# Windowed attention and a highway layer on one core: the t bias in four pieces beside the shifted value matmuls, merged exponentials, masks and copies from block 7 on, and a new order table

## The chip, the core and the metric

The kernel runs on 1 core of a Trainium2 chip. The metric is the device time of one execution in microseconds. Engines named below: PE (TensorE matmul), DVE (VectorE), ACT (ScalarE), POOL (GpSimd) and SP (SyncE). Before the change, 13 runs had a median of 120.59 us, from 119.31 to 123.08.

## What is computed

Attention over a sliding window with four sink positions, for 4 batches, 8 heads, 768 positions and 64 columns a head; its output, as 3072 tokens of 512 columns, goes through one highway layer.

```python
scores = scale * np.matmul(q, k.transpose(0, 1, 3, 2))
is_sink = pos[None, :] < n_sink                       # n_sink = 4
rel = pos[:, None] - pos[None, :]
in_window = (rel >= 0) & (rel < window)               # window = 128
scores = np.where(is_sink | in_window, scores, -1e9)
a = softmax(scores);  x = np.matmul(a, v)             # x as [3072, 512]
H = np.maximum(x @ w_h, 0.0)
T = 1.0 / (1.0 + np.exp(-(x @ w_t + b_t)))
out = T * H + (1.0 - T) * x
```

## The kernel before

The tokens are cut into 24 blocks of 128, six to a batch. The keys of block n are held in a chunk that is shifted by 64 positions, so that a block needs its own chunk in full and a half of the chunk on either side. Every block n goes through the same steps, each named by a letter in the order table and defined in the table STEP (L652):

- Loads: q, k and v of a block come through POOL's queue (L112, L119, L126), 128 KB each. The first ones stand in a fixed list (L210 to L238), the two weight matrices wh_sb and wt_sb (512 KB each, L191) among them. The later ones are issued inside the step A: A:n issues v of n+4, q and k of n+6 (L636).
- Tq, Tk: PE transposes of q or k into a PSUM tile (L323); tq, tk (ACT) or tqV, tkV (DVE) copy them out (L328). From block 3 on, the transposes are made inside S of an earlier block and stand in unused columns of that block's score tile ("hosted", L607). In and after block 9 one ACT copy, tt (L335), takes out both.
- S: the scores, the block's own chunk (L376) and the two half chunks (L389), into two PSUM tiles of two banks, each holding half of the heads. From block M0 = 9 on they are one tile of four banks with a single buffer (L295).
- x0_, x1_: the exponential of each half (ACT, L398); from block 9 on one xx for both (L403). m0_, m1_ and mm multiply with the window's mask (DVE, L409).
- sk, es: scores of the sink positions and their exponential (PE L358, ACT L365).
- A: the value product into the PSUM tile av, of which there is one. First the shifted value matmuls (L434), 16 of 64x64 operands and 66 columns: they use only the two quarters of the PE array that connect the lower rows with the upper columns and the other way round. Then the block's own chunk (L453) and the sinks (L459).
- xh: reciprocal of the denominators and the normalized block (DVE, L467 and L472). X transposes it back into av (PE, L486); xT (ACT) or xTV (DVE) copies that out (L491), after which the next block's A may overwrite av.
- Mh and Mt: the products with w_h (L514) and w_t (L502), four matmuls of 512 columns, into one of two PSUM banks m0 and m1. Which bank the n-th user gets is written out in the string M_BANKS.
- u: the tanh of the t half (ACT, L507). d, U, e and o (DVE, L520, L526, L531, L536) combine the two; o also issues the store on SP. The last block is done in two halves (Ta, Ha, ..., pb).

The t bias b_t is added on PE: a product of a row of ones with the bias row opens the accumulation group of Mt. For blocks 0 to 7 it is one matmul over the full array just ahead of Mt (L499). From B0 = 9 on, the step A of block n begins with the bias of block n-1 (pe_bias, L440), two matmuls of 64x64 operands and 512 columns, in the two quarters that the shifted value matmuls leave free. ones_row holds the ones of the first kind, ones2 those of the second.

The whole order is written by hand, in one table ORDER (L676): every engine takes its instructions in the order of this table and waits only for what its operands need. A step that waits holds back everything behind it on its engine. wA are idle matmuls at the start, which keep PE active.

Of the kernel before, what the change touches and what calls it, by code (L numbers as in the profile page):

```python
# [8 lines left out]
FP16 = mybir.dt.float16  # L9
# [11 lines left out]
def kernel(  # L21
# [18 lines left out]
    nc = tc.nc  # L40
# [49 lines left out]
    B0 = 9  # L90
    M0 = 9
# [52 lines left out]
    ones2 = const.tile([P, P], FP16, tag="ones2")  # L144
# [48 lines left out]
    with tc.manual_schedule(engines={ENG.Pool, ENG.SP}):  # L193
# [16 lines left out]
        load_q(3)  # L210
        load_k(2)
        load_q(4)
        load_q(1)
        load_k(3)
        load_q(2)
        load_v(2)
        load_k(5)
# [6 lines left out]
        load_k(4)  # L224
        load_v(3)
        load_w(moe_w_h, wh_sb)
        load_q(5)
        load_k(6)
        load_w(moe_w_t, wt_sb)
        load_v(4)  # L230
        load_q(6)
        load_k(7)
# [29 lines left out]
    def bias_rows(_):  # L262
        nc.vector.memset(bt16, 0.0)
        nc.vector.memset(ones_row, 0.0)
        nc.vector.memset(ones_row[0:1, :], 1.0)
        nc.vector.tensor_copy(out=ones2, in_=ones_row)
        nc.vector.memset(ones2[HP:HP + 1, :], 1.0)
# [5 lines left out]
    def sink_ones(_):  # L273
# [6 lines left out]
        "010101010101010101010101010010100101001100101011010110101101"  # L280
# [146 lines left out]
    def pe_AB(n):  # L427
        av = av_tile(n)
        nxt = v_ring[vi(n + 1)]
        prv = v_ring[vi(n - 1 if n % NSC else n)]  # L430
        lo, hi = slice(0, HP), slice(HP, P)
        for j in range(H):
            for src, part, vt, h in ((lo, hi, nxt, j), (hi, lo, prv, (j + 4) % H)):
                nc.tensor.matmul(  # L434
                    av[part, h // 4, h % 4, 0:_AVN], lhsT=e_at(n, h)[src, P:EW],
                    rhs=vt[src, 65 * h:65 * h + _AVN], start=(h % 4 == 0), stop=False,
                    skip_group_check=True)

    def pe_bias(n):
        t_of[n] = m_tile()  # L440
        for rows in (slice(0, HP), slice(HP, P)):
            nc.tensor.matmul(t_of[n][rows, :], lhsT=ones2[rows, rows], rhs=bt16[rows, :],
                             start=True, stop=False, skip_group_check=True)

    def pe_A(n):
        if n >= B0:
            pe_bias(n - 1)
# [229 lines left out]
    mz0_:0 ma:0 na:0 Tq:0 na:1 Tk:0 tq:0 mz1_:0 tk:0 ma:1 wA:0 wA:0 Tk:1 mc:0 cv:0 tk:1 fa:0  # L677
    wA:0 wA:0 wA:0 S:0 cv:1 x0_:0 fb:0 x1_:0 wA:0 wA:0 wA:0 wA:0 Tq:3 m0_:0 fc:0 tq:3 wA:0 Tk:2
    tk:2 m1_:0 fd:0 wA:0 wA:0 wA:0 wA:0 Tq:1 A:0 tq:1 S:1 xh:0 sk:1 x0_:1 x1_:1 Tq:2 m0_:1 X:0
    sk:3 xTV:0 es:1 Tk:3 m1_:1 tq:2 tk:3 wA:1 A:1 es:3 S:2 xh:1 x0_:2 x1_:2 Tk:4 m0_:2 sk:2  # L680
    tkV:4 X:1 es:2 m1_:2 S:3 xT:1 A:2 x0_:3 Mh:1 x1_:3 xh:2 tq:4 d:1 X:2 tk:5 Mh:0 xTV:2 m0_:3
    Mh:2 d:0 m1_:3 S:4 d:2 Mt:0 x0_:4 x1_:4 m0_:4 A:3 u:0 m1_:4 Mt:1 tq:5 xh:3 tk:6 U:0 sk:4 u:1
    e:0 S:5 es:4 o:0 X:3 x0_:5 U:1 sk:5 xTV:3 e:1 A:4 x1_:5 m0_:5 o:1 tq:6 Mt:2 xh:4 tk:7 es:5
    u:2 m1_:5 X:4 S:6 xT:4 U:2 e:2 A:5 x0_:6 o:2 Mh:3 x1_:6 xh:5 tq:7 Mh:4 m0_:6 tk:8 m1_:6 X:5
    d:3 S:7 xT:5 d:4 A:6 x0_:7 Mh:5 xh:6 x1_:7 Mt:3 d:5 tq:8 tk:9 m0_:7 X:6 u:3 m1_:7 Mt:5 xT:6
    U:3 e:3 sk:7 o:3 u:5 Tq:9 es:7 U:5 Mt:4 tq:9 e:5 o:5 S:8 u:4 U:4 A:7 x0_:8 e:4 o:4 Mt:6
    x1_:8 xh:7 tq:10 Mh:6 m0_:8 tk:10 m1_:8 u:6 X:7 d:6 S:9 xT:7 U:6 A:8 e:6 xx:9 o:6 sk:9 xh:8
    Mh:7 es:9 tt:9 mm:9 Mt:7 d:7 X:8 u:7 S:10 xTV:8 U:7 A:9 e:7 xx:10 o:7 Mt:8 xh:9 tt:10 Mh:8
    mm:10 u:8 X:9 d:8 S:11 xT:9 U:8 A:10 e:8 xx:11 o:8 sk:11 xh:10 Mt:9 es:11 tt:11 mm:11 Mh:9
    u:9 X:10 d:9 S:12 xT:10 U:9 A:11 e:9 xx:12 o:9 Mt:10 xh:11 tt:12 Mh:10 mm:12 u:10 X:11 d:10  # L690
    S:13 xT:11 U:10 A:12 e:10 xx:13 o:10 sk:13 xh:12 Mt:11 es:13 tt:13 mm:13 Mh:11 u:11 X:12
    d:11 S:14 xT:12 U:11 A:13 e:11 xx:14 o:11 Mh:12 xh:13 tt:14 Mt:12 mm:14 X:13 d:12 u:12 S:15
    xT:13 U:12 e:12 xx:15 A:14 o:12 sk:15 xh:14 Mt:13 tt:15 mm:15 es:15 X:14 S:16 u:13 xTV:14
    U:13 A:15 xx:16 Mh:14 xh:15 tt:16 Mt:14 d:14 mm:16 Mh:13 u:14 U:14 sk:17 d:13 X:15 es:17
    S:17 xT:15 e:13 e:14 A:16 xx:17 o:13 o:14 Mt:15 xh:16 tt:17 Mh:15 mm:17 u:15 X:16 S:18 d:15
    xT:16 U:15 A:17 xx:18 e:15 o:15 Mh:16 xh:17 tt:18 Mt:16 mm:18 X:17 u:16 S:19 xTV:17 d:16
    A:18 xx:19 U:16 e:16 sk:19 xh:18 Mt:17 es:19 mm:19 tt:19 Mh:17 o:16 u:17 X:18 S:20 d:17
    xT:18 U:17 A:19 xx:20 e:17 o:17 Mh:18 xh:19 tt:20 Mt:18 mm:20 X:19 u:18 S:21 xTV:19 d:18
    A:20 xx:21 U:18 e:18 sk:21 o:18 Mt:19 es:21 xh:20 tt:21 Mh:19 mm:21 u:19 X:20 S:22 d:19
    xT:20 U:19 A:21 xx:22 e:19 o:19 Mh:20 xh:21 tk:24 Mt:20 mm:22 X:21 u:20 S:23 xTV:21 d:20  # L700
    A:22 xx:23 U:20 e:20 sk:23 xh:22 Mt:21 es:23 mm:23 X:22 u:21 Mh:21 xT:22 o:20 A:23 d:21 U:21
    Mt:22 xh:23 e:21 X:23 u:22 Mh:22 xTV:23 o:21 Ta:23 d:22 Ha:23 ua:23 U:22 e:22 Tb:23 da:23
    o:22 Hb:23 ub:23 db:23 ea:23 eb:23 pa:23 pb:23
# [43 lines left out]
```

## Time and profile before

| | us |
|---|---|
| median of 13 runs | 120.59 |
| the profiled execution | 120.56 |
| its span, first to last instruction | 118.5 |
| outside the span | 2.06 |
| first scores, S:1 | from 13.86 |
| S:5 | from 29.34 |
| S:9 | from 48.30 |
| last store's computation ends | 115.1 |

The PE clock was granted in full in all 40 slices but the last. The page's durations of PE instructions include the pipeline: a matmul of 512 columns is shown with 379 ns, but four in a row take 0.86 us. So two PE instructions that overlap in the list are the normal case, and start times say more than durations. DVE's and ACT's instructions overlap by about 0.08 and 0.10 us in the same way. "Idle before" in brackets is the time that an engine had nothing to do before an instruction, with what ended it. DMA queues carry 17.64 MB over the span; the mean time from issue to landing is 5.6 to 6.3 us for a tile of q, k or v.

### The profile page before, as it was taken

Reading aid. Unit: us, or ns where it says so; the run is one execution under the profiler, and the core shown is the slowest. Engines: PE = TensorE matmul, PEld = TensorE weight load, DVE = VectorE, ACT = ScalarE, POOL = GpSimd, SP = SyncE. Lnnn points to the kernel's source line nnn. Section 1 sums busy time; section 2 is a strip of 40 time slices with the busy share of each in tenths; the row PEclk is TensorE's granted clock in tenths of the full one; section 3 lists DMA queues with packets and bytes.
Section 4 is the critical chain, followed back from the end, with each engine's and each line's share of the span. In section 5 each row is a group of like instructions: output and inputs, shape, how many; then the busy total and the mean of one; then the engine's idle time right before and its main releaser. Section 6 shows DMA issues by size and latency. Waiting matters only on the chain.

```text
span 118.5 us, 4975 instructions
## 1 busy us (share of the span) xinstructions
PE 107.1 (90%) x2119; PEld 65.4 (55%) x2119; DVE 103.3 (87%) x254; ACT 87.4 (74%) x123; POOL 72.1 (61%) x97
## 2 busy tenths in 40 slices
PE   5998777999899999999999989999999999999920
PEld 1433555556655556755765556757656665565610
DVE  6889847588989897999999999879999999999990
ACT  2249397929978978979989969897888979783210
POOL 5999886859799129976959838887694320000000
PEclk9999999999999999999999999999999999999995
DMA  2999999999999969999999999999899995112132
GB/s 60 217 168 152 148 173 175 196 155 153 121 229 198 159 58 193 184 148 202 192 180 156 141 196 172 193 131 113 133 197 187 176 138 115 44 50 84 50 132 89
DMA packets 79848, 17.64 MB, mean 149 GB/s; under 512 B 75602, under 2 KB 76882, under 8 KB 79828
## 3 DMA queue, kind: packets, MB, share of 16 engines
q0 software_dynamic: 71888, 9.97, 134.6%
q1 hardware_dynamic: 6884, 7.12, 19.4%
q10 hardware_dynamic: 1056, 0.26, 1.4%
q8 instruction: 16, 0.26, 0.9%
q14 instruction: 4, 0.03, 0.1%
HBM read 21.01 MB, written 6.29 MB: 230 GB/s over the span
## 4 chain that ended last, share of the span: by engine, by line
PE 53%; DVE 23%; DMA 6%; ACT 6%; issue 5%; POOL 3%; DVEq 0%; ACTq 0%
PE m L514 11%; PE m L502 10%; DMA qsd<-in_q_dram 6%; PE av L453 6%; DVE xh L472 5%; PE av L434 5%; DVE otok L536 5%; DVE e L409 3%; PE sps L323 3%; PE av L486 3%; PE sps L389 3%; ACT e L398 3%; PE sps L376 3%; PE av L459 3%; DVE dd L520 3%
## 5 line engine op out<-in xcount | busy, mean ns | idle before, releaser
L126 POOL DMA_DIRECT2D v<-in_v_dram x26 | 22.0, 849 | 13.8 <-PE av L434 10.7
L403 ACT ACTIVATE e<-sps,ebias 128x1536 f16<-128x1536 f32 x15 | 23.1, 1541 | 3.8 <-PE sps L389 3.5
L409 DVE TENSOR_TENSOR e<-e,mask 128x768 f16<-128x768 f16 (+1 forms) x33 | 23.9, 732 | 2.2 <-ACT e L398 2.2
L112 POOL DMA_DIRECT2D qsd<-in_q_dram x23 | 20.8, 905 | 5.4 <-PE sps L323 5.4
L502 PE MATMUL m<-wt_sb,xT 128*128 128x512 f16 x92 | 23.6, 379 | 0.0
L514 PE MATMUL m<-wh_sb,xT 128*128 128x512 f16 x92 | 23.3, 379 | 0.0
L119 POOL DMA_DIRECT2D ksd<-in_k_dram x26 | 22.1, 853 | 1.0 <-DVE otok L536 0.6
L398 ACT ACTIVATE e<-sps,ebias 128x768 f16<-128x768 f32 x18 | 15.3, 898 | 5.1 <-PE sps L389 4.8
L507 ACT ACTIVATE u<-m 128x512 f16<-128x512 f32 x23 | 13.7, 596 | 6.7 <-PE m L502 6.5
L472 DVE TENSOR_TENSOR xh<-av,rec 128x512 f16<-128x512 f32 x24 | 16.6, 691 | 0.8
L536 DVE SCALAR_TENSOR_TENSOR otok<-xh,ee 128x512 f32<-128x512 f16 x23 | 15.8, 689 | 0.6
L520 DVE SCALAR_TENSOR_TENSOR dd<-m,xh 128x512 f16<-128x512 f32 x23 | 15.7, 685 | 0.0
L514 PEld LDWEIGHTS <-xT 128*128 128x128 f16 x92 | 8.7, 98 | 8.6 <-issue 0.4
L502 PEld LDWEIGHTS <-xT 128*128 128x128 f16 x92 | 8.7, 98 | 8.0
L335 ACT COPY tt<-sps 128x1024 f16<-128x1024 f16 x13 | 13.0, 997 | 0.0
L434 PE MATMUL av<-v,e 64*64 64x66 f16 x384 | 10.9, 193 | 0.9 <-DVE xT L491 0.3
L328 ACT COPY t<-sps 128x512 f16<-128x512 f16 x19 | 10.4, 590 | 1.6 <-PE sps L323 1.6
L434 PEld LDWEIGHTS <-e 64*64 64x64 f16 x384 | 9.8, 107 | 2.9 <-issue 2.0
L531 DVE TENSOR_TENSOR ee<-u,dd 128x512 f16<-128x512 f16 x23 | 10.0, 439 | 0.7
L453 PE MATMUL av<-v,e 128*128 128x66 f16 x192 | 10.4, 196 | 0.0
L486 PEld LDWEIGHTS <-xh 64*128 64x128 f16 x192 | 4.2, 95 | 9.5 <-DVE xh L472 6.8
L491 ACT COPY xT<-av 128x512 f16<-128x512 f16 x15 | 8.7, 581 | 1.0 <-PE av L486 0.7
(94 smaller groups left out, 171.5 us busy)
## 6 DMA issues: line engine op xcount, KB each, us to landing
out_dram<-otok SPq DMA_DIRECT2D x23, 256.0 KB, 3.6
qsd<-in_q_dram POOLq DMA_DIRECT2D x23, 128.0 KB, 5.6
ksd<-in_k_dram POOLq DMA_DIRECT2D x19, 128.0 KB, 6.3
v<-in_v_dram POOLq DMA_DIRECT2D x19, 128.0 KB, 5.8
wh_sb<-in_moe_w_h_dram POOLq DMA_DIRECT2D x1, 512.0 KB, 8.4
wt_sb<-in_moe_w_t_dram POOLq DMA_DIRECT2D x1, 512.0 KB, 9.0
ksd<-in_k_dram POOLq DMA_DIRECT2D x7, 64.0 KB, 5.7
v<-in_v_dram POOLq DMA_DIRECT2D x7, 64.0 KB, 5.9
```

The lines of the kernel that those rows point to most:

```text
L112: nc.gpsimd.dma_start(out=qsd, in_=q[b, :, c * P:(c + 1) * P, :].transpose([1, 0, 2]))
L119: nc.gpsimd.dma_start(out=ksd[rows], in_=k[b, :, s0:s0 + nr, :].transpose([1, 0, 2]))
L126: nc.gpsimd.dma_start(out=vt[rows, :, 0:D], in_=v[b, :, s0:s0 + nr, :].transpose([1, 0, 2]))
L398: nc.scalar.activation(out=e_tile(n)[:, g].rearrange("p a b c -> p a (b c)"), in_=s_tile(n, g)[:, :, 0:2 * EW], func=AF.Exp, bias=ebias, s ...
L403: nc.scalar.activation(out=e_tile(n).rearrange("p g a b c -> p (g a) (b c)"), in_=s_of[n][:, :, 0:2 * EW], func=AF.Exp, bias=ebias, scale= ...
L409: nc.vector.tensor_tensor(out=ev, in0=ev, in1=m.unsqueeze(1).to_broadcast([P, k, EW]), op=ALU.mult)
L434: nc.tensor.matmul(av[part, h // 4, h % 4, 0:_AVN], lhsT=e_at(n, h)[src, P:EW], rhs=vt[src, 65 * h:65 * h + _AVN], start=(h % 4 == 0), sto ...
L472: nc.vector.tensor_tensor(out=xh.rearrange("p (h d) -> p h d", d=D), in0=av_of.pop(n)[:, :, 0:D], in1=rec_of.pop(n).unsqueeze(2).to_broadc ...
L502: nc.tensor.matmul(t_of[n], lhsT=xT[:, kc, :], rhs=wt_sb[:, kc, :], start=False, stop=(kc == NOC - 1), skip_group_check=True)
L514: nc.tensor.matmul(hps, lhsT=xT[:, kc, :], rhs=wh_sb[:, kc, :], start=(kc == 0), stop=(kc == NOC - 1))
L520: nc.vector.scalar_tensor_tensor(out=dd, in0=h_of.pop(n), scalar=0.0, in1=xh_of[n], op0=ALU.max, op1=ALU.subtract)
L536: nc.vector.scalar_tensor_tensor(out=otok, in0=xh_of.pop(n), scalar=2.0, in1=ee_of.pop(n), op0=ALU.mult, op1=ALU.add)
```

## The change

- Bias: pe_bias and ones2 go. In the new table T_BESIDE block n of A names the block m whose bias is opened in it. The bias is cut in four pieces of 128 columns, each as two 64x64 matmuls, issued after the first, third, fifth and seventh pair of shifted value matmuls. It holds t of blocks 2 (in A:3), 0 (A:4), 4 (A:6), 6 (A:7), and n-1 for A:8 to A:23. Blocks 1, 3 and 5 keep the full-array matmul ahead of Mt. ones_row now holds the ones in row 0 for the first 64 columns and in row 64 for the others, which serves both kinds.
- M0 goes from 9 to 7: blocks 7 and 8 use the four-bank score tile, and so xx, tt and mm.
- The first loads on POOL stand in another order.
- ORDER is new, and with it the string M_BANKS.

```diff
-    B0 = 9
-    M0 = 9
+    T_BESIDE = {3: 2, 4: 0, 6: 4, 7: 6, 8: 7, 9: 8, 10: 9, 11: 10, 12: 11, 13: 12, 14: 13, 15: 14, 16: 15, 17: 16, 18: 17, 19: 18, 20: 19, 21: 20, 22: 21, 23: 22}
+    M0 = 7
...
-        load_q(3)
-        load_k(2)
-        load_q(4)
         load_q(1)
         load_k(3)
+        load_k(2)
+        load_k(6)
         load_q(2)
         load_v(2)
-        load_k(5)
+        load_q(3)
+        load_k(4)
+        load_v(3)
...
-        load_k(4)
-        load_v(3)
+        load_q(4)
+        load_k(5)
+        load_q(5)
+        load_v(4)
         load_w(moe_w_h, wh_sb)
-        load_q(5)
-        load_k(6)
         load_w(moe_w_t, wt_sb)
-        load_v(4)
+        load_k(7)
         load_q(6)
-        load_k(7)
         load_v(5)
...
         nc.vector.memset(ones_row, 0.0)
-        nc.vector.memset(ones_row[0:1, :], 1.0)
-        nc.vector.tensor_copy(out=ones2, in_=ones_row)
-        nc.vector.memset(ones2[HP:HP + 1, :], 1.0)
+        nc.vector.memset(ones_row[0:1, 0:HP], 1.0)
+        nc.vector.memset(ones_row[HP:HP + 1, HP:P], 1.0)
...
-        "010101010101010101010101010010100101001100101011010110101101"
+        "010101010100101101011010110101010110101100101011010110101101"
...
+        m = T_BESIDE.get(n)
+        if m is not None:
+            t_of[m] = m_tile()
         for j in range(H):
             for src, part, vt, h in ((lo, hi, nxt, j), (hi, lo, prv, (j + 4) % H)):
                 nc.tensor.matmul(
                     av[part, h // 4, h % 4, 0:_AVN], lhsT=e_at(n, h)[src, P:EW],
                     rhs=vt[src, 65 * h:65 * h + _AVN], start=(h % 4 == 0), stop=False,
                     skip_group_check=True)
-
-    def pe_bias(n):
-        t_of[n] = m_tile()
-        for rows in (slice(0, HP), slice(HP, P)):
-            nc.tensor.matmul(t_of[n][rows, :], lhsT=ones2[rows, rows], rhs=bt16[rows, :],
-                             start=True, stop=False, skip_group_check=True)
+            if m is not None and j % 2 == 0:
+                cols = slice(D * j, D * j + 2 * D)
+                for part in (lo, hi):
+                    nc.tensor.matmul(
+                        t_of[m][part, cols], lhsT=ones_row[part, part], rhs=bt16[part, cols],
+                        start=(j == 0), stop=False, skip_group_check=True)
 
     def pe_A(n):
-        if n >= B0:
-            pe_bias(n - 1)
         pe_AB(n)
```

The order tables are 461 and 456 steps long. Here are the stretches that the prediction speaks of: the start, up to S:5, and blocks 13 to 16.

```diff
-    mz0_:0 ma:0 na:0 Tq:0 na:1 Tk:0 tq:0 mz1_:0 tk:0 ma:1 wA:0 wA:0 Tk:1 mc:0 cv:0 tk:1 fa:0
-    wA:0 wA:0 wA:0 S:0 cv:1 x0_:0 fb:0 x1_:0 wA:0 wA:0 wA:0 wA:0 Tq:3 m0_:0 fc:0 tq:3 wA:0 Tk:2
-    tk:2 m1_:0 fd:0 wA:0 wA:0 wA:0 wA:0 Tq:1 A:0 tq:1 S:1 xh:0 sk:1 x0_:1 x1_:1 Tq:2 m0_:1 X:0
-    sk:3 xTV:0 es:1 Tk:3 m1_:1 tq:2 tk:3 wA:1 A:1 es:3 S:2 xh:1 x0_:2 x1_:2 Tk:4 m0_:2 sk:2
-    tkV:4 X:1 es:2 m1_:2 S:3 xT:1 A:2 x0_:3 Mh:1 x1_:3 xh:2 tq:4 d:1 X:2 tk:5 Mh:0 xTV:2 m0_:3
-    Mh:2 d:0 m1_:3 S:4 d:2 Mt:0 x0_:4 x1_:4 m0_:4 A:3 u:0 m1_:4 Mt:1 tq:5 xh:3 tk:6 U:0 sk:4 u:1
-    e:0 S:5 es:4 o:0 X:3 x0_:5 U:1 sk:5 xTV:3 e:1 A:4 x1_:5 m0_:5 o:1 tq:6 Mt:2 xh:4 tk:7 es:5
+    mz0_:0 ma:0 na:0 na:1 wA:0 wA:0 Tk:0 mz1_:0 Tq:0 tk:0 ma:1 tq:0 mc:0 Tk:1 cv:0 tk:1 fa:0
+    wA:0 wA:0 wA:0 S:0 fb:0 x0_:0 cv:1 x1_:0 wA:0 wA:0 wA:0 wA:0 Tq:1 m0_:0 tq:1 m1_:0 wA:0 wA:0
+    wA:0 Tk:2 Tk:3 tk:2 tkV:3 fc:0 wA:0 wA:0 S:1 A:0 x0_:1 fd:0 xh:0 x1_:1 Tq:2 sk:1 tq:2 m0_:1
+    es:1 m1_:1 Tq:3 X:0 tq:3 xTV:0 sk:3 S:2 es:3 sk:2 x0_:2 x1_:2 wA:1 wA:1 Tk:4 m0_:2 A:1 tkV:4
+    es:2 m1_:2 S:3 xh:1 x0_:3 X:1 xTV:1 x1_:3 m0_:3 A:2 tq:4 m1_:3 tk:5 xh:2 X:2 sk:4 xT:2 Mh:1
+    es:4 S:4 d:1 A:3 x0_:4 x1_:4 Mt:2 xh:3 tq:5 Mt:1 m0_:4 u:2 m1_:4 tk:6 U:2 Mh:0 u:1 U:1 X:3
+    d:0 S:5 xT:3 e:1 sk:5 x0_:5 o:1 A:4 es:5 m0_:5 x1_:5 Mh:2 xh:4 tq:6 Mt:0 m1_:5 tk:7 d:2 X:4
...
-    S:13 xT:11 U:10 A:12 e:10 xx:13 o:10 sk:13 xh:12 Mt:11 es:13 tt:13 mm:13 Mh:11 u:11 X:12
-    d:11 S:14 xT:12 U:11 A:13 e:11 xx:14 o:11 Mh:12 xh:13 tt:14 Mt:12 mm:14 X:13 d:12 u:12 S:15
-    xT:13 U:12 e:12 xx:15 A:14 o:12 sk:15 xh:14 Mt:13 tt:15 mm:15 es:15 X:14 S:16 u:13 xTV:14
-    U:13 A:15 xx:16 Mh:14 xh:15 tt:16 Mt:14 d:14 mm:16 Mh:13 u:14 U:14 sk:17 d:13 X:15 es:17
+    Mt:11 xh:12 tt:13 sk:13 mm:13 u:11 X:12 S:14 xT:12 U:11 es:13 xx:14 A:13 Mh:11 xh:13 tt:14
+    Mt:12 d:11 mm:14 sk:15 u:12 X:13 es:15 S:15 xTV:13 e:11 A:14 xx:15 U:12 o:11 Mt:13 xh:14
+    tt:15 Mh:12 mm:15 u:13 X:14 d:12 S:16 xT:14 e:12 A:15 xx:16 U:13 o:12 Mh:13 xh:15 tt:16
+    Mt:14 d:13 mm:16 X:15 u:14 Mh:14 xT:15 e:13 U:14 sk:17 d:14 S:17 es:17 o:13 A:16 xx:17 e:14
```

In the new table DVE has the copies tkV:3, tkV:4, tqV:9 and xTV of blocks 0, 1, 4, 6, 13, 17, 19, 21 and 23; before, tkV:4 and xTV of 0, 2, 3, 8, 14, 17, 19, 21 and 23.

## The prediction, made before the changed kernel ran

> **What bounds the kernel now.** I read the page from the top: the busy times, then the busy time by stretch, then the chain of waits, then the timeline of one engine at a time where these pointed.
>
> ```profile
> PE 107.1 (90%) x2119; PEld 65.4 (55%) x2119; DVE 103.3 (87%) x254; ACT 87.4 (74%) x123; POOL 72.1 (61%) x97
> ```
>
> No engine stands out, so a share of the span says little. The windows cut the run at DVE's first score mask (11.73 us), at 29.0 and at the reciprocals of blocks 9 and 23 (54.64, 108.99). Columns: stretch, length, busy us (instructions) of PE, weight loads, DVE, ACT, POOL, then PE clock, DMA, GB/s.
>
> ```profile
> 54.64:108.99 54.35, 53.56 (x1152) 33.79 (x1151) 51.85 (x101) 46.69 (x58) 28.71 (x37) 1.00 1.39 143
> 11.73:29.00 17.27, 15.01 (x324) 9.35 (x322) 12.12 (x27) 11.94 (x21) 13.60 (x17) 1.00 2.24 168
> 29.00:54.64 25.64, 24.76 (x530) 15.66 (x529) 23.39 (x51) 21.90 (x36) 19.50 (x25) 1.00 1.98 164
> ```
>
> DVE's idle time is 5.15 us in the start, 2.25 in the middle, 2.50 in the long regular part. PE records are pipelined, so PE's 0.8 us of idle in the last stretch is not all its slack. From 29 us on, the kernel is bound by PE and DVE together, and what can be won is idle time of both. DVE's timeline says where it lies (brackets: idle before, and who ended it).
>
> ```profile
> 22.02 0.21 DVE L467 RECIPROCAL rec<-av 128x8 f32<-128x8 f32 x1 [1.25 <-PE av L459]
> ...
> 45.37 0.29 DVE L526 TENSOR_SCALAR u<-u 128x512 f16<-128x512 f16 x1 [0.51 <-ACT u L507]
> ...
> 77.74 0.21 DVE L467 RECIPROCAL rec<-av 128x8 f32<-128x8 f32 x1 [0.93 <-PE av L459]
> ```
>
> **Part 1, the bias.** PE's timeline around block 9's shifted value matmuls (L434), and around block 19's:
>
> ```profile
> 53.33 0.38 PE L442 MATMUL m<-bt,ones 64*64 64x512 f16 x1
> 53.34 0.20 PE L434 MATMUL av<-v,e 64*64 64x66 f16 x2
> 53.34 0.38 PE L442 MATMUL m<-bt,ones 64*64 64x512 f16 x1
> 53.37 0.39 PE L434 MATMUL av<-v,e 64*64 64x66 f16 x14
> 53.70 0.43 PE L453 MATMUL av<-v,e 128*128 128x66 f16 x8
> ...
> 92.97 0.39 PE L442 MATMUL m<-bt,ones 64*64 64x512 f16 x2
> 93.12 0.45 PE L434 MATMUL av<-v,e 64*64 64x66 f16 x16
> ```
>
> At 53.33 the two bias halves and the value matmuls start within 0.01 us of each other and the full-array matmuls follow 0.37 later. So the four 64x64 quarters of the array already work at once. At 92.97 the bias runs while L434 waits for the copy of xT, which ACT's timeline has from 92.48 for 0.58 (to 93.06). For t of blocks 8 to 22, 15 pairs, the bias costs nothing today, and moving it gains nothing. What it costs as eight pieces of 128 columns: four 512-column matmuls take 0.86 in the chain, so 512 columns are 0.216 and a piece 0.054. Four on each quarter are 0.22, beside eight value matmuls per quarter that take 0.26 to issue: 0. If the two halves had to take turns, 8 x 0.054 = 0.43, that is 0.17 more a block. I take 0, by the row at 53.33.
>
> [...]
>
> Five full-array biases in front of Mt (L499, t of blocks 0, 2, 4, 6, 7) go: 5 x 0.216 = 1.08 us of PE, all before 52 us. The chain holds four L499 pieces (0.22, 0.22, 0.32, 0.38), so some of it counts; it is inside the walk below. A bias piece also waits for its m bank, and behind it in PE's queue stand the rest of that A step and the next product. I followed the bank string: the nearest readers are es:4 before A:3 and es:17 before A:16, each with a whole S step (0.7 us) between, against 0.35 for es. I take 0.
>
> **Part 2, merging blocks 7 and 8.** ACT: two half exponentials take 1.69 and two copies 1.07, merged 1.54 and 1.00, so 0.22 saved a block; ACT has slack, 0. DVE: two half masks occupy 0.93 until the next instruction, a merged one 0.87: 2 x 0.07 = 0.14 saved. Price: the first mask begins 0.64 later (after 1.54, not 0.90), and S:8 waits for tt:7, as the merged tile has one buffer. PE has two products queued between, so I take -0.14, with +0.6 as the other end.
>
> **Part 3, setup and copies on DVE.** The copy to ones2 and its memset go: 7.92 to 8.49, 0.57, less about 0.15 for the new one-row memset. DVE's early queue is full, so the first mask moves from 11.73 to 11.3. DVE takes 12 PSUM copies instead of 10: +2 x 0.34 = +0.67, one of them before 29 us.
>
> **Part 4, the start.** Chain: q1, fourth in POOL's queue, was issued at 5.54 and landed 7.31 later, at 12.85; PE sat idle for it. k2, second, was needed and there at 10.94. That is about 0.97 a place. Now q1 is first and k2 third (11.9). I walk the new order with the rows' durations, from 11.9: both k transposes and copies to 12.8; S:1 12.8 (was 13.86); its half exponentials end 15.1 (16.19); S:2 16.9 (17.82), ends of its exponentials 19.2 (20.19); S:3 19.5 (20.24), 22.1 (22.86). So the attention is about 0.9 us ahead. But A:1 and norm 1 now stand behind S:2 and Tk:4: reciprocal 19.7, where it was 17.92; and A:2 is at 21.5 (20.95).
>
> Then the weights. The DMA issue rows of the page:
>
> ```profile
> wh_sb<-in_moe_w_h_dram POOLq DMA_DIRECT2D x1, 512.0 KB, 8.4
> wt_sb<-in_moe_w_t_dram POOLq DMA_DIRECT2D x1, 512.0 KB, 9.0
> ```
>
> Issued at 12.33 and 15.94, they landed at 20.7 and 24.9. From q1's 12.85 to 20.7 lie six tiles and wh, ten tiles of bytes, 0.79 each. The new queue puts three more tiles before wh and one more before wt: about 23.1 and 25.7. Mh:1 ran at 21.82; now it stands behind X:2 (23.6), so at about 23.9, and S:4 behind it at 24.8 (25.07). By then the old order had three products done, the new one has one. Walking on: A:3 25.5, Mt:2, Mt:1, Mh:0, S:5 at 29.3 (29.34), with four products done against five, and DVE about 1.4 us behind in d, U, e and o. The start is therefore not a gain by itself: the lead in attention pays for work put off.
>
> **Part 5, the middle.** With that work in hand DVE should not run dry. Its work from d:0 (29.65) to the reciprocal of block 9, by start-to-start times: eight e and o with six U, 8 x 1.39 - 0.5 = 10.6; four half and three merged masks 4.46; five norms at 0.84, 4.2; seven d at 0.60, 4.2; three copies 1.0; less 0.12 at four places where a step no longer follows the one it needs. Sum 24.0, so 53.65 with no idle time, 55.9 with the 2.25 of today. I take 0.4 idle: 54.05 against 54.64, -0.6.
>
> The steps that move carry transfers: A:n loads v, q and k on POOL, tk:6 the two L347 copies and L186 (1.03), o its store on SP. POOL's order of these is the same in both; it waited for tk:6 until 31.4, now about 28.9. Today POOL also idles 4.7 us before the load of q12 (43.63) for Tq:9, which moves forward. Nothing of this is on the path; 0 to -0.3, taken as 0.
>
> **Part 6, the regular part.** PE and DVE lists are alike except from block 12 to 17. There the old list lets DVE wait 0.93 at 77.74 with nothing before it but xTV:14 and U:13; the new one puts d:12, e:12, U:13, o:12 there, 2 us of work. I take -0.8 of the 0.93 (ends 0 and -1.2, the latter with the slow pair of e at 81.13, which took 1.10 where two take 0.88).
>
> **Sum.** -0.6 - 0.8 = -1.4 us. The profiled execution took 120.56 us around its span of 118.5, and the median is 120.59, so 119.2 us.
>
> **Rivals.**
> - *The gain in full.* DVE never idles in the middle (another -0.4), the whole 1.2 of part 6 comes, and a quarter of the saved 1.08 of PE shows where PE is the bound (-0.3): -2.5, 118.1. For it: PE and DVE were never both idle for long after 29 us. Against: a wait that goes usually uncovers the next.
> - *No net gain.* The work put off at the start is only caught up, and DVE idles in the middle as today: 55.9 against 54.64 is +1.3, less 0 to 1.2 later: 120.6 to 121.9, taken as 121.0. For it: S:4 to S:9 hang on wh's landing, which is an estimate, one for one. Against: DVE has more in its queue than before.
> - *The bias halves take turns, slower.* Place: the L434 group of A:3 to A:23. Price 0.17 x 20 = 3.4 us of PE; the regular part has PE at 53.56 of 54.35, so the 0.8 left hides little, and with the gain of 1.4 the result is 121.8 to 122.6, taken as 122.3. It decides once a block takes over 0.07 us more than today (1.4 / 20). Against it is the row at 53.33.
> - *wh late, slower.* A microsecond or two behind 23.1, S:4 and everything after it moves as much: 120.6 to 122.6, taken as 121.5.
>
> **Chances.** What a measurement of this kernel can tell from no change is about 1%, so 119.4 to 121.8 is the same. The forecast case gets 0.38 (its own range is 118.4 to 120.1; 0.23 of it lies below 119.4), the full gain 0.19, no net gain 0.17 (0.02 below 119.4 by part 6's end, 0.04 above 121.8), turns 0.15 (0.13 above), late loads 0.11 (0.07 above). Faster 0.23 + 0.19 + 0.02 = 0.44, slower 0.04 + 0.13 + 0.07 = 0.24, same 0.32. The range, 117.8 to 122.1, leaves out a fifth of the full gain (0.04), two thirds of turns (0.10) and some of late loads (0.05).
>
> **What would show it.** S:1 near 12.8 and Mh:1 near 24 confirm the start; the reciprocal of block 9 near 54 the middle; no DVE wait near 0.9 us around block 15 the regular part. L434 to L453 at 0.38 in every block shows the bias free; 0.55 shows turns. I am wrong if wh lands after 24, if DVE's idle time from 29 us on is not below 3.5 us, or if PE's time from A to X grows by a tenth of a microsecond.

## The result and the profile after

The changed kernel took 122.79 us at the median of 11 runs (121.95 to 126.19), the kernel before 120.63 over 48 runs beside them. The ratio is 1.0197, 95% interval 1.0157 to 1.0237: about 2% slower. The prediction was 119.2 us, from 117.8 to 122.1. Ratios in this text leave out executions more than 1.5% above the fastest of their kernel (8 of 12 for b_count below, 7 of 12 for b_s48), so a ratio can differ from that of two medians. The profiled execution took 121.71 us (span 119.7), below every timed run; a second one, taken later, took 123.82 (span 122.0). So the first profile shows only part of the loss, and the second is needed too.

The page's busy line of the changed kernel, first profile:

```profile
PE 103.9 (87%) x2245; PEld 64.0 (53%) x2245; DVE 102.9 (86%) x253; ACT 86.5 (72%) x117; POOL 72.8 (61%) x97
```

PE and DVE are both busy for less time than before, by 3.2 and 0.4 us, and the span is 1.2 longer: the time is in waits. The windows, cut at the same work as before (DVE's first mask, 29.0, the reciprocals of blocks 9 and 23):

```profile
10.87:29.00 18.13, 13.96 (x338) 9.21 (x339) 11.77 (x28) 12.57 (x22) 14.95 (x20) 1.00 2.26 164
29.00:55.16 26.16, 24.81 (x569) 15.58 (x568) 24.27 (x50) 21.21 (x30) 19.63 (x24) 1.00 2.08 167
55.16:110.22 55.06, 52.91 (x1232) 33.24 (x1231) 51.74 (x102) 46.30 (x57) 28.80 (x36) 1.00 1.33 139
```

The reciprocal of block 9 comes 0.52 later than before, and the regular part takes 55.06 where it took 54.35. DVE idles in it for 3.3 us, before for 2.5. The lines that answer to those of before, from DVE's timeline (22.44 is block 2, 55.16 block 9, 78.45 block 15), then the two weight loads from the page:

```profile
22.44 0.20 DVE L466 RECIPROCAL rec<-av 128x8 f32<-128x8 f32 x1
...
55.16 0.20 DVE L466 RECIPROCAL rec<-av 128x8 f32<-128x8 f32 x1
...
78.45 0.21 DVE L466 RECIPROCAL rec<-av 128x8 f32<-128x8 f32 x1 [0.40 <-PE av L458]
```

```profile
wh_sb<-in_moe_w_h_dram POOLq DMA_DIRECT2D x1, 512.0 KB, 7.1
wt_sb<-in_moe_w_t_dram POOLq DMA_DIRECT2D x1, 512.0 KB, 8.9
```

**A wait that has no cause in the kernel.** The view of PE's waits has rows that end in "issue": PE waited for nothing that the profile shows. In the first profile after (us in total, times, longest):

```profile
PE av L435 <- issue: 1.2, 2, 0.8
PE m L442 <- issue: 0.6, 1, 0.6
PE sps L387 <- issue: 0.3, 1, 0.3
```

PE's timeline in A:4 shows what such a wait looks like:

```profile
30.79 0.22 PE L442 MATMUL m<-bt,ones_row 64*64 64x128 f16 x1
30.79 0.19 PE L435 MATMUL av<-v,e 64*64 64x66 f16 x1
31.82 0.22 PE L435 MATMUL av<-v,e 64*64 64x66 f16 x2 [0.82 <-issue]
31.84 0.24 PE L442 MATMUL m<-bt,ones_row 64*64 64x128 f16 x2
```

In the midst of one group of 24 matmuls, whose operands have long been there and of which ten have started, nothing starts for 1.03 us. DVE waits 0.82 for it at 32.80. The profile of before has the same thing in S:2:

```profile
18.14 0.31 PE L389 MATMUL sps<-t,t 64*64 64x64 f16 x13
19.02 0.22 PE L389 MATMUL sps<-t,t 64*64 64x64 f16 x3 [0.57 <-issue]
```

I counted the rows of the trace on PE (matmuls, weight loads and the few semaphore instructions) in order of start. A gap is the time from one start to the next. From 6 us on, all gaps over 0.32 us at full clock that end in "issue" stand at one place of that count; shorter ones, up to 0.32 us, stand elsewhere too:

```
profile            PE rows   gaps over 0.32 us without a releaser: row (us)               sum
before                4281   449 (0.76)  961 (0.45)  2497 (0.74)                          1.95
after, first          4532   961 (1.03)  2497 (0.58)  3009 (0.46)  3777 (0.84)            2.92
after, second         4532   961 (1.36)  2497 (1.11)  3777 (1.11)                         3.58
```

Every one is a row 193 + 256 k. The page's DMA table has a queue named "instruction", before and then after:

```profile
q8 instruction: 16, 0.26, 0.9%
```

```profile
q8 instruction: 17, 0.28, 1.0%
```

16 packets of 0.26 MB in all are 16 KB each; 4281 rows over 256 are 16.7, and after the change 17 packets stand against 17.7. The reading that fits is that one packet holds the next 256 PE instructions; no row of a trace says what a packet holds. By it, in all gaps of these profiles the packet began 81 to 144 rows ahead of its first instruction, and that instruction started no sooner than 2.2 us after the packet began (2.19 at row 2497 of the first profile after). The same holds for all 303 boundaries of the 19 usable profiles: none is crossed sooner than 2.18 us after its packet began. PE passes 128 rows of X, S and A in some 1.5 us (at row 2497 of the first profile after, 144 rows in 1.6, the gap left out); by this reading it can wait if the boundary falls there. Of the 16 boundaries from row 449 on in the first profile after, 12 have no gap over 0.01 us; the other four have 0.46 to 1.03 us each.

**The clock.** The second profile has a row that the first has not: windows around 16 us, the third value from the end is the granted PE clock:

```profile
15.00:16.50 1.50, 0.60 (x20) 0.40 (x18) 1.50 (x4) 1.50 (x4) 1.50 (x3) 1.00 2.19 131
16.50:19.70 3.20, 3.04 (x42) 1.75 (x41) 0.62 (x2) 2.08 (x5) 3.20 (x5) 0.50 2.02 136
```

PE, which had been busy for 0.60 of 1.5 us, ran at half clock for 3.4 us from 16.5 on. The reciprocal of block 2 was 1.44 us later than in the first profile.

### The profile page after: what moved, and what is told of

Same layout as the page of the kernel before. It is cut to its first block, busy times and chain, and to the rows that moved or that the text cites. A ratio compares the mean times of both kernels' runs of the same rounds, so it can differ in the third digit from the quotient of the medians.

```text
span 119.7 us, 5217 instructions
## 1 busy us (share of the span) xinstructions
PE 103.9 (87%) x2245; PEld 64.0 (53%) x2245; DVE 102.9 (86%) x253; ACT 86.5 (72%) x117; POOL 72.8 (61%) x97
## 4 chain that ended last, share of the span: by engine, by line
PE 42%; DVE 34%; ACT 7%; DMA 6%; issue 5%; POOL 2%; DVEq 0%; ACTq 0%
PE m L513 9%; PE m L501 7%; DVE e L407 7%; DVE xh L471 6%; DVE otok L535 6%; DMA ksd<-in_k_dram 6%; PE av L452 4%; DVE ee L530 4%; PE sps L321 4%; DVE dd L519 4%; PE av L435 3%; ACT e L396 3%; PE m L356 3%; DVE u L525 3%; PE sps L387 3%
## 5 line engine op out<-in xcount | busy, mean ns | idle before, releaser
L401 ACT ACTIVATE e<-sps,ebias 128x1536 f16<-128x1536 f32 x17 | 26.2, 1540 | 4.2 <-PE sps L387 3.9
L407 DVE TENSOR_TENSOR e<-e,mask 128x1536 f16<-128x1536 f16 (+1 forms) x31 | 23.5, 768 | 2.2 <-ACT e L396 2.2
L501 PE MATMUL m<-wt_sb,xT 128*128 128x512 f16 x92 | 23.6, 379 | 0.0
L513 PE MATMUL m<-wh_sb,xT 128*128 128x512 f16 x92 | 23.5, 379 | 0.0
L396 ACT ACTIVATE e<-sps,ebias 128x768 f16<-128x768 f32 x14 | 11.9, 895 | 4.3 <-PE sps L387 4.2
L333 ACT COPY tt<-sps 128x1024 f16<-128x1024 f16 x15 | 15.0, 999 | 0.0
L435 PE MATMUL av<-v,e 64*64 64x66 f16 x384 | 11.1, 193 | 2.6 <-issue 1.2
L435 PEld LDWEIGHTS <-e 64*64 64x64 f16 x384 | 9.5, 107 | 4.0 <-issue 3.0
L452 PE MATMUL av<-v,e 128*128 128x66 f16 x192 | 10.4, 195 | 0.0
L442 PE MATMUL m<-bt,ones_row 64*64 64x128 f16 x160 | 8.6, 221 | 0.6 <-issue 0.6
```

The costliest lines, as they stand in the source:

```text
L396: nc.scalar.activation(out=e_tile(n)[:, g].rearrange("p a b c -> p a (b c)"), in_=s_tile(n, g)[:, :, 0:2 * EW], func=AF.Exp, bias=ebias, s ...
L401: nc.scalar.activation(out=e_tile(n).rearrange("p g a b c -> p (g a) (b c)"), in_=s_of[n][:, :, 0:2 * EW], func=AF.Exp, bias=ebias, scale= ...
L407: nc.vector.tensor_tensor(out=ev, in0=ev, in1=m.unsqueeze(1).to_broadcast([P, k, EW]), op=ALU.mult)
L435: nc.tensor.matmul(av[part, h // 4, h % 4, 0:_AVN], lhsT=e_at(n, h)[src, P:EW], rhs=vt[src, 65 * h:65 * h + _AVN], start=(h % 4 == 0), sto ...
L501: nc.tensor.matmul(t_of[n], lhsT=xT[:, kc, :], rhs=wt_sb[:, kc, :], start=False, stop=(kc == NOC - 1), skip_group_check=True)
L513: nc.tensor.matmul(hps, lhsT=xT[:, kc, :], rhs=wh_sb[:, kc, :], start=(kc == 0), stop=(kc == NOC - 1))
```

## The experiments

Two theories stood at the outset. F: the waits for instructions cost the time, through where each 256th row falls and how many rows there are. O: the new order (or S, its start; R, its regular part) or the bias pieces (P) cost it by themselves. C, the clock at the start, came with the second profile.

**Moving the count alone.** Idle warm-up matmuls at the start are cut into column pieces, so that the rows ahead of everything grow and nothing else changes. more is 16 in a_s16, 80 in a_s80, and in the kernel before 48, 24 and 6 (b_s48, b_s24, b_s6).

```diff
-        for _ in range(n):
-            nc.tensor.matmul(w, lhsT=warm[:, 0:P], rhs=warm, start=True, stop=True)
+        more = 16
+        for i in range(n):
+            cuts = more // n + (i < more % n) + 1
+            edges = [DM * c // cuts for c in range(cuts + 1)]
+            for a, b in zip(edges, edges[1:]):
+                nc.tensor.matmul(w[:, a:b], lhsT=warm[:, 0:P], rhs=warm[:, a:b], start=True,
+                                 stop=True)
```

a_s16: 

> The changed kernel with 16 more TensorE matmuls: two of the idle warm-up matmuls at the start are cut into nine column pieces each, the columns are the same. Nothing from 5 us on changes but the count of TensorE instructions ahead of it (32 more rows). Theory F (TensorE waits for its own instructions at each 256th row, where a dense stretch runs into the boundary): all boundaries fall 32 rows earlier in the order; the sum of these stalls falls from 2.9 us in the profile to about 1.2, the time to about 121.3 us (ratio to before 1.006, between 1.000 and 1.012). Theory O (the order of the start and the middle, or the bias pieces, cost the time): nothing moves, ratio 1.020 within 0.004.

a_s80: 

> As the kernel with 16 more matmuls, with 80 more (160 rows), cut out of the same warm-up columns. Theory F: the boundaries fall on the dense stretches of blocks more often, seven places instead of four; stalls about 4 us in the profile, time about 123.5 us (ratio 1.022 to 1.032), and at least 1.5 us above the kernel with 16 more. Theory O: 1.020 within 0.004, as the kernel with 16 more.

b_s48: 

> The kernel before, with 48 more TensorE matmuls (96 rows) cut out of the warm-up columns in the same way; order, bias and masks are untouched. Theory F: stalls at the 256th rows rise from 2.0 us in the profile to about 3.2, time to about 121.8 us (ratio 1.006 to 1.015). Theory O: ratio 1.000 within 0.004.

Measured: 1.0247 (1.0182 to 1.0313), 1.0244 (1.0169 to 1.0320) and 1.0094 (1.0035 to 1.0153). The kernel before becomes 0.9% slower by nothing but 96 more rows ahead of it: gaps at 705, 2497, 3009 and 3521, 2.77 us in sum. That is F's number, and O has none for it. The cut columns cost nothing where they stand: DVE's first mask begins at 11.73 in the profile before and at 11.74 in that of b_s48. But in the changed kernel F missed twice. With 16 more it did not become faster, as F had expected, and with 80 more it is not 1.5 us above that; the two ratios are as O would have them, a little high. The profile of a_s16 lacked the gaps at 961 and 2497, had 1.81 us at row 1985 instead, where the packet began only 39 rows ahead, and then half clock from 56.6 us on. My reckoning of where a gap will be, from the stretches of a trace, is not good enough to aim with.

**The pieces back to a pair.** The bias of the same blocks in two matmuls of 512 columns ahead of the value matmuls.

```diff
+            for part in (lo, hi):
+                nc.tensor.matmul(
+                    t_of[m][part, :], lhsT=ones_row[part, part], rhs=bt16[part, :],
+                    start=True, stop=False, skip_group_check=True)
         for j in range(H):
...
-            if m is not None and j % 2 == 0:
-                cols = slice(D * j, D * j + 2 * D)
-                for part in (lo, hi):
...
```

a_pair: 

> The changed kernel with the bias of the same blocks as two matmuls of 512 columns ahead of the value matmuls, as before, instead of eight of 128 between them. Theory P (the pieces themselves lengthen A): ratio falls to 1.005 or less. Theory F: 240 fewer TensorE rows move the boundaries, but the sum of the stalls by the stretches of the profile stays near the changed kernel's (boundaries in six dense stretches): ratio 1.013 to 1.022. Theory O alone: the pair costs what the pieces hid, at most 20 x 0.1 us more than the changed kernel, ratio 1.020 to 1.035.

Measured: 1.0198 (1.0124 to 1.0271). Its profile (120.92 us, the fastest of its runs) has one gap, 0.99 at row 961. So undoing the pieces does not by itself bring the time back, and P alone is out; F and O both allowed this ratio.

**Halves of the change.** The order is cut at S:10, where both kernels stood at about 51.5 us once their gaps are taken out. h_AB takes the changed loads, start and order up to there, h_BA the changed order from there on, with the pieces; b_pieces takes only the pieces. In h_AB the bias is a pair from block 10 on. The diff is that of h_BA and b_pieces against the kernel before, where pe_bias goes; the orders are put together from the two tables.

```diff
+        m = n - 1 if n >= B0 else None
...
+            if m is not None and j % 2 == 0:
+                cols = slice(D * j, D * j + 2 * D)
+                for part in (lo, hi):
+                    nc.tensor.matmul(
+                        t_of[m][part, cols], lhsT=ones2[part, part], rhs=bt16[part, cols],
+                        start=(j == 0), stop=False, skip_group_check=True)
```

h_AB: 

> The changed kernel's loads, start and order up to S:10 (with the merged blocks 7 and 8 and the pieces there), then from S:10 on the order of the kernel before, with the bias of blocks 9 to 22 as the pair of 512 columns. Theory S (the start and the middle cost the 2%): ratio 1.015 to 1.022. Theory R (the regular part costs it: its order and the pieces): 1.000 within 0.005. Theory F (stalls at the 256th TensorE rows, by where they fall; by the stretches of both traces put together 3.6 us at most against 3.3 of before and 6.0 of the change): 1.000 to 1.008.

h_BA: 

> The opposite: the loads, the start and the order of the kernel before up to S:10, then the changed order with the pieces from A:9 on. Theory S: 1.000 within 0.005, or below by the 0.8 us that the regular part was to gain (0.993). Theory R: 1.015 to 1.022. Theory F (4.1 us of stalls at most by the same reckoning): 1.003 to 1.012.

b_pieces: 

> The kernel before with one edit: the bias of blocks 8 to 22 in pieces of 128 columns between the shifted value matmuls, in place of the pair ahead of them; its order is unchanged. Theory P (the pieces cost time where they stand): 1.010 or more. Theory F: 180 more TensorE rows by the end; 4.2 us of stalls at most, 1.003 to 1.012, and the gaps in the profile at rows 193 + 256 k alone. Prediction's own step (the pieces are hidden beside the value matmuls): 1.000 to 1.003.

a_again: 

> The changed kernel as it is, with a second profile. All theories: 1.020 within 0.005. Theory F: in a profile near the median of 122.8 us the gaps at rows 193 + 256 k add up to more than the 2.9 us of the first profile (121.7 us), by about the difference of the two times; other theories: the difference lies elsewhere, in DMA or VectorE waits.

Measured: h_AB 1.0078 (1.0022 to 1.0134), h_BA 1.0114 (1.0067 to 1.0160), b_pieces 1.0138 (1.0031 to 1.0245), the change again 1.0238 (1.0163 to 1.0314). Neither S alone nor R alone holds: each half costs about one per cent, which is what F had for both. b_pieces by its ratio lies in P's range and a little above F's. The second profile of the change has 3.58 us of gaps for 2.92, as F expected, but the larger part of its 2.2 us more is the clock, which F did not foresee. In the profile of h_AB the loss is there too, half clock from 17.4 us on.

**Filling the start, and the order without the pieces.** a_fill and a_pair_fill put six idle matmuls where PE waits between 10 and 16.5 us (the diff, whose rows of the order table are cut short at both ends); h_BAp is the kernel before with the changed order, and its M_BANKS, from S:10 on and nothing else.

```diff
-    wA:0 Tk:2 Tk:3 tk:2
+    wA:0 wA:0 wA:0 Tk:2 Tk:3 tk:2
-    m1_:1 Tq:3 X:0 tq:3 xTV:0 sk:3 S:2
+    m1_:1 wm:1 wm:1 Tq:3 X:0 tq:3 xTV:0 wm:1 wm:1 sk:3 S:2
+        "wm": lambda n: spare(m_bank[n]),
```

a_fill: 

> The changed kernel with six more idle matmuls of 512 columns where TensorE waits between 10 and 16.5 us (two ahead of Tk:2, two ahead of Tq:3, two ahead of sk:3), and the bias of A:3 as the pair, which takes six matmuls away, so that from A:3 on every instruction has its old place in the count. Theory C (in part of the executions the granted clock falls to 0.5 for 3 us at 16.6 us, as in the second profile of the change and in that of its start with the old rest, because TensorE idles too much between 10 and 16.5 us): the clock stays at 1.00, ratio to before falls from 1.020-1.024 to 1.010-1.015, the spread of the times shrinks; the gap at row 961 stays near 1 us. Theory F alone: ratio stays at 1.018 to 1.024. Theory S' (the fills delay the start): above 1.024.

a_pair_fill: 

> The changed kernel with the bias as the pair of 512 columns everywhere, and the same six idle matmuls at the start. Its profile without them had one gap of 1 us and took 120.9 us, its median was 122.5. Theory C: the median comes down to the good profile, 120.9 to 121.5, ratio 1.003 to 1.010. Without C: 1.017 to 1.022 as without the fills.

h_BAp: 

> The kernel before with one edit: the order from S:10 on is the changed one; the bias stays a pair, so the number of TensorE instructions is that of before, and so are loads, start and merged blocks. Prediction's step on the regular part (the VectorE wait of 0.93 us goes): 0.993 to 0.996. Theory F: the gain is given back by the stalls, which by the stretches put together are up to 0.8 us more: 0.997 to 1.004. If the pieces are what cost the time in the kernel with the old start and the new rest (1.011): at or below 1.000 here, 1 per cent apart from it.

b_s24: 

> The kernel before with 24 more TensorE matmuls (48 rows) cut out of the warm-up columns; half of what cost 0.9 per cent before. Theory F: by the stretches of the trace the boundaries fall best near here (1.7 us of stalls at most against 3.3 of before and 5.5 with 48 more matmuls): ratio 0.990 to 1.001, below the kernel with 48 more by 0.8 per cent or more. If cutting the warm-up costs time by itself: 1.004 to 1.006, half of the cost with 48.

Measured: a_fill 1.0202 (1.0135 to 1.0268), a_pair_fill 1.0159 (1.0079 to 1.0239), h_BAp 1.0013 (0.9971 to 1.0054), b_s24 1.0136 (1.0080 to 1.0193). Six fills did not do what C said. In the profile of a_fill the clock held, but in that of a_pair_fill it fell at 23.6 us, behind the next wait that had no fill. h_BAp says that the changed regular order costs nothing, and gains nothing, as long as the bias stays a pair; its interval shuts out the predicted gain of 0.8 us (0.993). b_s24 is a miss for my reckoning, which had called that place the best one. Its profile has a single large gap, 1.63 us at row 2241. That 48 rows cost over half a per cent with nothing else changed stands all the same, though the sum of gaps in its one profile, 2.01, is that of before: the rest of its loss is not seen there.

**Count or place.** b_count has the count of the pieces without their place, b_mid the place without the count; the first half of the diff is b_count, in pe_bias, the second b_mid, in pe_AB. h_ABp is h_AB with the pair everywhere.

```diff
-        for rows in (slice(0, HP), slice(HP, P)):
-            nc.tensor.matmul(t_of[n][rows, :], lhsT=ones2[rows, rows], rhs=bt16[rows, :],
-                             start=True, stop=False, skip_group_check=True)
+        for j in range(0, H, 2):
+            cols = slice(D * j, D * j + 2 * D)
+            for rows in (slice(0, HP), slice(HP, P)):
+                nc.tensor.matmul(t_of[n][rows, cols], lhsT=ones2[rows, rows], rhs=bt16[rows, cols],
+                                 start=(j == 0), stop=False, skip_group_check=True)
...
+            if m is not None and j == 3:
+                for part in (lo, hi):
+                    nc.tensor.matmul(
+                        t_of[m][part, :], lhsT=ones2[part, part], rhs=bt16[part, :],
+                        start=True, stop=False, skip_group_check=True)
```

b_count: 

> The kernel before with the bias of blocks 8 to 22 as eight matmuls of 128 columns, all of them ahead of the value matmuls, none between: as many TensorE instructions, in as many columns, as with the pieces between (which took 1.014), but no interleaving. Theory F (the count matters, by where each 256th instruction falls): 1.010 to 1.018. Theory P (the place between the value matmuls costs the time): 1.000 to 1.005.

b_mid: 

> The kernel before with the pair of 512-column bias matmuls of blocks 8 to 22 in the middle of the shifted value matmuls (after the fourth head) instead of ahead of them: interleaved, but with the count of instructions of before. Theory F: 1.000 within 0.005. Theory P: 1.008 to 1.014.

b_s6: 

> The kernel before with 6 more warm-up matmuls (12 rows), which gives it at S:10 and at the end the count of the changed kernel with the pair. If the 2.0 per cent of that kernel are the shift of its count: 1.012 to 1.020. If they are its start: 1.000 to 1.006. By the stretches of the trace of before, 3.6 us of stalls at most against 3.3 unshifted.

h_ABp: 

> The changed loads, start and order up to S:10, with the merged blocks 7 and 8, then the order of before; the bias is a pair everywhere. With the regular order of no weight (1.001 with the start of before), Theory S (the start costs the 2 per cent): 1.015 to 1.022, as the whole change with the pair. Theory F: the time follows the count, as the kernel before with 6 more warm-up matmuls does, within 0.006 of it.

Measured: b_count 1.0065 (1.0002 to 1.0127), b_mid 1.0031 (0.9983 to 1.0079), b_s6 1.0050 (1.0000 to 1.0100; its profiled execution took 523.9 us and is not used), h_ABp 1.0127 (1.0059 to 1.0195). b_mid shows the place to be harmless: P expected 1.008 or more, and the profile has no gap at all. b_count lies between the two theories by its ratio; its median, 123.68 for 121.00, is on F's side, its ratio alone does not settle it. b_s6 has the 1.005 that was expected if the count of the kernel with the pair is not what costs it its 2%. h_ABp fits neither S (1.015 or more) nor F. Its profile has no gap either and yet ends 1.22 us later than before; with the count of b_s6 it is 0.8% above that kernel, so the start does cost something that is not the count, though the two intervals overlap. Windows of h_ABp, then of the next experiment's h_ABp_fill:

```profile
10.00:15.00 5.00, 3.84 (x89) 2.31 (x89) 4.08 (x11) 3.32 (x6) 4.33 (x7) 1.00 2.85 145
15.00:21.00 6.00, 4.80 (x96) 3.13 (x98) 2.87 (x7) 3.61 (x8) 6.00 (x8) 0.72 2.13 158
```

```profile
10.00:15.00 5.00, 4.03 (x85) 2.28 (x82) 4.18 (x11) 2.99 (x6) 4.84 (x8) 1.00 2.92 146
15.00:21.00 6.00, 5.80 (x138) 3.50 (x137) 3.59 (x10) 4.26 (x9) 6.00 (x8) 1.00 2.03 168
```

A clock of 0.72 over 6 us is 3.4 us at one half. With 13 fills PE is busy for 5.80 of 6 us instead of 4.80, and the clock holds.

**The clock against the count, at one count.** h_ABp_fill is h_ABp with idle matmuls in all waits of PE from 10 to 23.5 us (the diff, rows cut short as above); h_ABp_s13 is h_ABp with 13 more matmuls cut out of the warm-up columns, as above.

```diff
-    wA:0 Tk:2 Tk:3 tk:2
+    wA:0 wA:0 wA:0 Tk:2 Tk:3 tk:2
-    m1_:1 Tq:3 X:0 tq:3 xTV:0 sk:3 S:2
+    m1_:1 wm:1 wm:1 Tq:3 X:0 tq:3 xTV:0 wm:1 wm:1 sk:3 S:2
-    x0_:3 X:1 xTV:1 x1_:3 m0_:3 A:2
+    x0_:3 wm:1 X:1 xTV:1 x1_:3 m0_:3 wm:1 wm:1 A:2
-    xh:2 X:2 sk:4
+    xh:2 wm:1 wm:1 wm:1 wm:1 X:2 sk:4
```

h_ABp_fill: 

> The changed start with the old rest and the pair of bias matmuls (1.013), with 13 idle matmuls of 512 columns put into all the waits of TensorE between 10 and 23.5 us: two ahead of Tk:2, Tq:3, sk:3 and A:2, one ahead of X:1, four ahead of X:2. Theory C: the granted clock stays at 1.00 through the start in the profile, and the ratio falls to 1.000 to 1.008, at least 0.5 per cent under the same kernel with the 13 matmuls' count but no fill. Without C: both between 1.008 and 1.018, within 0.4 per cent of each other. If the fills delay what stands behind them: above the other by up to 13 x 0.216 us = 2.8 us.

h_ABp_s13: 

> The changed start with the old rest and the pair, with 13 more matmuls cut out of the warm-up columns: the count of instructions of the kernel with the 13 fills, and no fill. Both theories: 1.008 to 1.018. Theory C: the granted clock falls to 0.5 at 15 to 21 us in the profile, if it falls in this execution (it did in three of six profiles of this start without a fill).

Measured: 1.0044 (1.0005 to 1.0084) and 1.0112 (1.0040 to 1.0184). The fill takes 0.7 to 0.8% off, against the equal count and against no fill (1.0127), as C said, though the intervals overlap. In the profile of h_ABp_s13 the clock was at half twice, for 3.4 us each, from 17.9 and from 24.7 us on.

Of the eight usable profiles with the changed start and no fill, four show half clock between 16 and 28 us; of eight with the start of before, one (b_count, 15.5 us). The record can say more than the profiles, since it has the mean clock of every execution: in the 19 profiles that is 0.985 or less where the clock fell during the work, and 0.989 or more where it fell only at the end. With the changed start and no fill 38 of 60 executions have 0.985 or less, with six fills 6 of 12, with 13 fills none of 12, the kernel before 28 of 106, and the versions with its start 15 of 83. So the 13 fills do hold the clock, and the kernel before loses it too, only less often. No version beat both kernels: h_BAp and b_mid equal the kernel before.

## Why the prediction was wrong

**What was right.** The start was walked correctly. The first mask was put at 11.3 and began at 10.87, S:1 was put at 12.8 and began at 12.47, the product Mh:1 at 23.9 and began at 23.88; wh was to land at 23.1 and landed at 22.93, wt at 25.7 and 25.47. From PE's timeline after:

```profile
12.47 0.40 PE L374 MATMUL sps<-t,t 64*128 64x128 f16 x8
...
23.88 1.03 PE L513 MATMUL m<-wh_sb,xT 128*128 128x512 f16 x4
```

**Part 1, the bias beside.** The step "I take 0" holds for what it was about. The first and last rows of one A, block 14:

```profile
73.31 0.20 PE L435 MATMUL av<-v,e 64*64 64x66 f16 x2
...
73.67 0.43 PE L452 MATMUL av<-v,e 128*128 128x66 f16 x8
```

L435 to L452 takes 0.36 to 0.40 us in 20 of the 23 blocks from 1 on, as before; the other three (0.97 to 1.40) hold a gap. The rival that the halves take turns, priced at 0.55, is out: it would have shown in every block. What failed is the sum of the step: a cost was looked for in columns and in waits, and none in the number of instructions. The change has 126 more matmuls, 251 more PE rows in the trace, nearly all in the densest stretch of a block. The kernels with pieces in the regular part and the kernels with a pair, by the length of that part (reciprocal of block 9 to that of block 23) and, in brackets, the gaps over 0.25 us at rows 193 + 256 k in it, all in us:

```
pair:    before 54.35 (0.74)   b_mid 54.03 (0)       h_ABp 53.71 (0)      h_ABp_fill 53.71 (0)
         h_AB 53.75 (0)        a_pair 53.92 (0)      h_BAp 54.20 (0)      h_ABp_s13 54.44 (0.86)
         b_s24 55.40 (1.63)    b_s48 55.73 (2.32)    a_pair_fill 55.81 (1.97)
pieces:  after 55.06 (1.88)    a_again 55.54 (2.22)  a_fill 54.61 (1.29)  a_s80 55.80 (2.33)
         b_pieces 55.31 (2.14) h_BA 55.35 (1.37)     b_count 55.76 (2.22) a_s16 55.98 (0.52, half clock)
```

All eight profiles with the count of the pieces have gaps there, 1.75 us in the mean; six of the eleven with the pair have none, and the mean of the eleven is 0.68. Against the shortest of the same order a microsecond of gaps costs 0.5 to 1.0 us. By the ratios the pieces' count costs about 0.8% (b_pieces 1.0138, h_BA 1.0114, b_count 1.0065, against b_mid 1.0031 and h_BAp 1.0013).

**Part 2, the merge** (-0.14) can't be told apart from the rest in these runs; it was not tried alone.

**Parts 4 and 5, start and middle.** The sum went wrong by 1.1 us: block 9 at 55.16 for 54.05. DVE's idle time in the middle was predicted at 0.4; one wait of 0.82, at 32.80, is the gap in A:4, so that by this reckoning three quarters of the error are the gap and 0.3 a wrong size. In a_fill that gap is 0.61 for 1.03 and block 9 comes at 54.72. Behind a part of the median's loss is another step, "I walk the new order with the rows' durations": the rows were those of one execution at a clock of 1.00, which was taken as given. The changed start leaves PE idle for longer (4.17 us from the first mask to 29.00 by the windows, before 2.26), and in four of its eight profiles without a fill the clock falls for 3.4 us. That costs about 1.4 us where it happens (h_ABp ends 1.41 after h_ABp_fill; the second profile after is 1.44 behind the first at block 2); holding the clock is worth some 0.7% by h_ABp_fill.

**Part 6, the regular part.** This step failed in its own reasoning. "I take -0.8 of the 0.93": the wait at block 15 did go (in a_fill there is none; the 0.40 here is the gap at row 3009), but a new one stands at block 13. DVE after:

```profile
68.76 0.28 DVE L525 TENSOR_SCALAR u<-u 128x512 f16<-128x512 f16 x1
70.26 0.21 DVE L466 RECIPROCAL rec<-av 128x8 f32<-128x8 f32 x1 [1.21 <-PE av L458]
70.50 0.69 DVE L471 TENSOR_TENSOR xh<-av,rec 128x512 f16<-128x512 f32 x1
```

and DVE before:

```profile
68.83 0.28 DVE L526 TENSOR_SCALAR u<-u 128x512 f16<-128x512 f16 x1
69.15 0.43 DVE L531 TENSOR_TENSOR ee<-u,dd 128x512 f16<-128x512 f16 x1
69.61 0.69 DVE L536 SCALAR_TENSOR_TENSOR otok<-xh,ee 128x512 f32<-128x512 f16 x1
70.48 0.21 DVE L467 RECIPROCAL rec<-av 128x8 f32<-128x8 f32 x1 [0.18 <-PE av L459]
```

The 2 us of work that the new table puts ahead of block 15 (d:12, e:12, o:12) is there because d:11, e:11 and o:11 were put behind block 13, where they had covered the wait for A:13. I had looked at where the work goes and not at where it is taken from. The wait there is 1.03 to 1.25 us in a_pair, a_fill and h_BAp too. With no gaps the old order needs 53.71 to 54.03, the changed one 53.92 to 54.20: no gain, h_BAp's 1.0013.

**The rivals.** None named the cause. By its number "turns" (122.3) is nearest, and its mechanism is out. "No net gain" (121.0) had DVE idle in the middle as before, 2.25 us; it was 1.89, nearer to that than to the forecast's 0.4, but with wh on time. Of the signs named, one came: DVE's idle time from 29 us on is not below 3.5 but 5.2 (1.89 and 3.32 by the windows). It pointed at waits, not at their cause. wh was not late, and from the start of A to that of X the median from block 9 on is 2.70 us, before 2.72.

**What adds up and what does not.** The account by ratios: the pieces' count 0.8%, the clock 0.7% against a start that never loses it, the regular order 0. These do not add up to the change's 2.0%. The kernel before loses the clock too, in 28 of 106 executions, so the clock is worth less than 0.7% between the two kernels: of the executions that the ratios count, those with a mean clock of 0.989 or more have a median of 121.97 us for the changed kernel (5) and 120.17 for the one before (62), so that 1.5% is left with the clock held. And a_pair loses its 1.0198 without any pieces. At least a third of the loss is thus tied neither to the clock nor to the pieces' count by any run. That it is gaps of the same kind, which the new start moves to other instructions, would fit b_s24 (48 rows alone, 1.0136), but is not shown. Why a packet begins 39 rows ahead at one time and 150 at another, and thus which boundary stalls, stays open too.

## What to carry to other kernels

Look through PE's waits for those that the profile ascribes to nothing: here they come at some of the places where a dense stretch of short matmuls crosses a 256th instruction (gaps of 0.46 to 1.03 us in the first profile after), and cutting one matmul into four cost about 0.8% here, though its columns were hidden. When a wait goes because work is moved in front of it, look for the place that the work was moved from. Where an order leaves PE waiting in its start, take more than one profile and look at the mean clock of every execution, since one may not show the clock fall; or fill all the waits (here, by the mean clock, it fell in 38 of 60 executions of the changed start without a fill and in none of 12 with 13 fills).

## What the runs showed of the hardware

- In 19 profiles, gaps of PE over 0.32 us at full clock that have no releaser stand, from 6 us on, at rows 193 + 256 k alone; the longest took 1.97 us (a_pair_fill, row 2753).
- The falls of the clock during the work, eight in seven profiles, lasted 3.41 us each, at 0.50. Each of the eight came a whole number of times 3.41 us (3, 4, 5, 6 or 15) after the clock's first record of 1.00, which was 4.3 to 7.2 us from the span's start, differing with the execution; the two of h_ABp_s13 came 6.8 us apart. Why one execution has a fall and another has none is not shown. In the 3.41 us ahead of a fall PE was busy for 1.5 to 2.4 us, but some stretches as light had no fall behind them.
- In a_s16 a fall came 0.8 us after the start that ended a gap of 1.81 us. Behind the longer gap of a_pair_fill there was none, so that one brings the other is not shown.
- A half mask on DVE that ran beside POOL's L186 took 1.39 us in h_BA, where it takes 0.56 elsewhere (1.39 beside L186 in b_count and b_s48 too). From the timeline of h_BA:

```profile
31.39 1.18 POOL L186 TENSOR_TENSOR vs<-vd,bm 32x512 f16<-32x512 f32 x1
...
31.60 1.39 DVE L409 TENSOR_TENSOR e<-e,mask 128x768 f16<-128x768 f16 x1
```
